# Attention then feed-forward on one core: longer score bursts, regrouped tail products, single PSUM banks and crossbar transposes

## The chip, the cores and the metric

One core of a Trainium2 chip runs one program. Times are device microseconds of an execution; most executions of a kernel agree within 0.3% to 1%. Lower is better. Every run here that is compared is of the fast state; one run of the kernel before took 1890.24 us and is left out of every comparison.

TensorE (PE) does matmuls and writes PSUM; VectorE (DVE) and ScalarE (ACT) evict PSUM; GpSimd (POOL) issues the loads, SyncE (SP) the stores and, in the changed kernel, the crossbar transposes. Each engine runs its instructions in program order (run 6 shows one holding up its queue for 4.72 us).

## The reference

```python
def _attn_ref(q, k, v):                          # (8 batches, 12 heads, 448 rows, 64)
    scores = (1 / np.sqrt(64)) * np.matmul(q, k.transpose(0, 1, 3, 2))
    attn = np.maximum(scores, 0.0) ** 2 / 448
    return np.matmul(attn, v)

def _moe_ref(x, w_gate, w_val, w_out):           # x (3584, 768), d_ff 1536
    return (np.maximum(x @ w_gate, 0.0) * (x @ w_val)) @ w_out
# reference: x is the attention result, heads side by side; output (3584, 768) float32
```

## The kernel before

Everything on TensorE is bf16. A *group* is four heads of a batch; there are 24. Per group: 28 small transposes of q and k on TensorE (T), seven score tiles S(0) to S(6), relu and square on ACT and DVE, then the products with v (PV). S(0) to S(5) use 64 rows x 128 columns of the array; S(6), the *tail* (448 = 3 x 128 + 64), uses 64x64 pieces. The main products use 128x64, their tails 64x64, feed-forward the whole 128x128. A small planner in the kernel simulates the engines and emits all instructions in the order of its planned starts. It puts *bursts* of attention between the feed-forward matmuls of the batch before.

```python
    def bank_pair(dt=FP32):          # all of PSUM: four pairs of banks, shared by every use
        return psum.tile([128, 2, 512 if dt == FP32 else 1024], dt, name="ps", tag="ps", bufs=4)
# ... cut ...
        def pv(self):                # main products, then the tail products
            for j in range(2):
                for c in range(NC):
                    for h2 in range(2):  # 12 matmuls, 128 rows x 64 columns
                        nc.tensor.matmul(x_ps[o, j, :S], ..., start=(c == 0), stop=False)
            for j, h2, half in ((0, 0, 0), (0, 1, 1), (1, 0, 1), (1, 1, 0)):
                nc.tensor.matmul(x_ps[o, j, :S], ..., start=False, stop=True)   # 64x64
# ... cut: gate and value of feed-forward share one pair, so do the two output halves ...
        nb += 1                      # nb counts bursts: four for a group
        att.append((qd.s(0), nb))
        att.append((qd.s(1), nb))
        nb += 1
        att.append((qd.s(2), nb))
        if not early: PV()           # of the group before; "early" is batch 0
        nb += 1
        att.append((qd.s(3), nb))
        if early: T(n + 1)
        att.append((qd.s(4), nb))
        if not early: T(n + 1)       # of the next group
        nb += 1
        att.append((qd.s(5), nb))
        if early: PV()
        att.append((qd.s(6), nb))
```

Of the kernel before, what the change touches and what calls it, by code (L numbers as in the profile page):

```python
# [12 lines left out]
ET = mybir.EngineType  # L13

# [17 lines left out]
class Op:  # L32
    def __init__(self, engs, emit, deps=(), alloc=(), reads=(), xfer=0.0):
        self.engs, self.emit = engs, emit
        self.deps, self.alloc, self.reads = list(deps), list(alloc), list(reads)
        self.xfer = xfer
        self.start = self.end = None


class Planner:  # L40
# [4 lines left out]
    def __init__(self):  # L45
        self.t = {}
        self.ops = []
        self.dmaq = 0.0
        self.landed = []

    def ready(self, op):
        r = 0.0
        for d in op.deps:
            if d.end is None:
                return None
            r = max(r, d.end + self.LAT)
        need = {}
        for b in op.alloc:
            need[b.res] = need.get(b.res, 0) + 1
        for res, n in need.items():  # L60
            if len(res.free) < n:
                return None
            r = max(r, sorted(res.free)[n - 1] + self.LAT)
        return r
# [12 lines left out]
    def commit(self, op, s, e):  # L77
# [4 lines left out]
        if op.xfer:  # L82
            if e == "POOL":
                self.dmaq = max(self.dmaq, op.end + 1.0) + op.xfer
                op.end = self.dmaq + 1.0
                self.landed.append(op.end)
            else:
                op.end += 2.0 + op.xfer
# [11 lines left out]
def plan(att, ffn, others, pool, nburst):  # L100
# [9 lines left out]
    while ai < len(att) or fi < len(ffn) or pend or pi < len(pool):  # L110
        cands = []
        for op in pend:
            b = P.best(op)
            if b is not None:
                cands.append((b[0], b[2], 1, b[1], op))
        if pi < len(pool):
            b = P.best(pool[pi])
            if b is not None:
# [3 lines left out]
                cands.append((s, 0.0, 0, "POOL", pool[pi]))  # L122
# [14 lines left out]
        if pick == "A":  # L137
            cands.append((A[0], A[2], 2, "PE", att[ai][0]))
        elif pick == "F":
            cands.append((F[0], F[2], 2, "PE", ffn[fi][1]))  # L140
        assert cands, "no operation can start"
        s, _, kind, e, op = min(cands, key=lambda c: c[:3])
# [23 lines left out]
def kernel(  # L166
# [36 lines left out]
    inp = ctx.enter_context(tc.tile_pool(name="inp", bufs=2))  # L203
    tpool = ctx.enter_context(tc.tile_pool(name="tpool", bufs=4))
# [8 lines left out]
    r_in, r_ps = Res(2), Res(4)  # L213
    r_t, r_r, r_at, r_x, r_h, r_g, r_o = Res(4), Res(4), Res(2), Res(2), Res(1), Res(4), Res(3)

    def bank_pair(dt=FP32):
        return psum.tile([128, 2, 512 if dt == FP32 else 1024], dt, name="ps", tag="ps", bufs=4)
# [9 lines left out]
    def dma_in(dst, src, n_desc, xfer, deps=(), alloc=()):  # L227
        op = Op({"POOL": 0.5 + 0.0004 * n_desc}, lambda: nc.gpsimd.dma_start(out=dst(), in_=src),  # L228
                deps=deps, alloc=alloc, xfer=xfer)
# [5 lines left out]
    def load_gv(c):  # L235
# [3 lines left out]
        wg_op[c] = dma_in(lambda: w_gate_sb[c], wg[:, :, cols], 768, 2.0)  # L239
        wv_op[c] = dma_in(lambda: w_val_sb[c], wv[:, :, cols], 768, 2.0)  # L240

    def load_out(c):
        wo = moe_w_out.rearrange("(kf p) m -> p kf m", p=128)
        wo_op[c] = dma_in(lambda: w_out_sb[c], wo[:, :, c * OH:(c + 1) * OH], 1536, 6.0)
# [11 lines left out]
    def load_heads(b, h0, n):  # L256
        if b not in bat:
            bat[b] = Batch()
            bat[b].buf = Buf(r_in, 1)
# [3 lines left out]
        def tiles():  # L263
            if not hasattr(st, "qk"):
                st.qk = inp.tile([128, H, NT, D], BF16, name="qk")
                st.vv = inp.tile([128, H, NC + 2, D], BF16, name="vv")
            return st
# [3 lines left out]
        al = [st.buf] if h0 == 0 else []  # L271
        k_op = dma_in(lambda: tiles().qk[64:128, hs], rows(k), 64 * n, 64 * n * 0.06 / 16, alloc=al)
        q_op = dma_in(lambda: st.qk[0:64, hs], rows(q), 64 * n, 64 * n * 0.06 / 16)
        v0 = dma_in(lambda: st.vv[0:64, hs, 1:NC + 2], rows(v)[:, :, 0:NC + 1], 64 * n, 64 * n * 0.045 / 16)
        v1 = dma_in(lambda: st.vv[64:128, hs, 0:NC + 1], rows(v)[:, :, NC:NT], 64 * n, 64 * n * 0.045 / 16)
        for h in range(h0, h0 + n):
            st.qk_op[h] = (k_op, q_op)
            st.v_op[h] = (v0, v1)
# [14 lines left out]
    def transpose_quad(b, g):  # L293

        st = bat[b]
        ps = Buf(r_ps, 2)
        box = {}

        def emit():
            t_ps = bank_pair(BF16)  # L300
            for j in range(2):
                for i, t in enumerate(slot_order(b)):
                    for h2 in range(2):
                        nc.tensor.transpose(t_ps[64 * h2:64 * h2 + 64, j, i * 128:(i + 1) * 128],  # L304
                                            st.qk[:, 4 * g + 2 * j + h2, t, :], ident)
            box["ps"] = t_ps

        def emit_copy(cp, j):
            box[j] = tpool.tile([128, 2, NT, P2], BF16, name="qk_sb")
            dst = box[j].rearrange("p a t c -> p t a c")  # L310
            src = box["ps"][:, j, :2 * S].rearrange("p (t a c) -> p t a c", t=NT, a=2)
# [6 lines left out]
        op = Op({"PE": 1.05}, emit, deps=deps, alloc=[ps])  # L318
        for j in range(2):
            sb = Buf(r_t, NC + 1)  # L320
            cp = Op({"DVE": 0.68, "ACT": 0.9}, None, deps=[op], alloc=[sb], reads=[ps])
# [11 lines left out]

    xop = {}

    class Quad:
# [6 lines left out]
        def s(self, i):  # L343
            b, g, box = self.b, self.g, self.box
            ps = Buf(r_ps, 1)
# [4 lines left out]
            def emit():  # L350
                if i == 0:
                    box["at"] = apool.tile([128, 2 * NC + 1, 2, S], BF16, name="at")
                s_ps = bank_pair()
                if i < 2 * NC:
                    _, q_of, k_of, _ = tr[0]
                    for h2 in range(2):
                        nc.tensor.matmul(s_ps[:, h2, :S], lhsT=k_of(h2, key_off(b) + (i % NC) * 128, 128),  # L357
                                         rhs=q_of(h2), start=True, stop=True)
                else:

                    for j, h2, half in ((0, 0, 0), (0, 1, 1), (1, 0, 1), (1, 1, 0)):
                        _, q_of, k_of, _ = tr[j]
                        nc.tensor.matmul(s_ps[64 * half:64 * half + 64, h2, :S],  # L363
                                         lhsT=k_of(h2, key_tail(b), P2), rhs=q_of(h2),
                                         start=True, stop=True)
                loc["s"] = s_ps

            op = Op({"PE": 0.25 if i < 2 * NC else 0.32}, emit, deps=[x[0] for x in tr],
                    alloc=[ps] + ([self.at_buf] if i == 0 else []), reads=[])
            for x in tr:  # L370
                sbuf = x[3]
                op.reads.append(sbuf)
            r = Buf(r_r, 1)

            def emit_relu(op_relu):
                loc["r"] = rpool.tile([128, 2, S], BF16, name="r_sb")
                if op_relu.eng == "ACT":
                    nc.scalar.activation(loc["r"], loc["s"][:, :, :S], AF.Relu)  # L378
                else:
                    nc.vector.tensor_scalar_max(loc["r"], loc["s"][:, :, :S], 0.0)  # L380

            relu = Op({"ACT": 0.92, "DVE": 1.12}, None, deps=[op], alloc=[r], reads=[ps])
            relu.emit = lambda: emit_relu(relu)
            sq = Op({"DVE": 0.63}, lambda: nc.vector.tensor_tensor(box["at"][:, i], loc["r"], loc["r"], ALU.mult),  # L384
                    deps=[relu], reads=[r])
            others.extend([relu, sq])
# [3 lines left out]
        def pv(self):  # L390
            b, g, box = self.b, self.g, self.box
            st = bat[b]
            ps = Buf(r_ps, 1)
            loc = {}

            def emit():
                x_ps = bank_pair()
                at = box["at"]
                for j in range(2):
                    for c in range(NC):  # L400
                        for h2 in range(2):
                            o = slice(64 * h2, 64 * h2 + 64)
                            nc.tensor.matmul(x_ps[o, j, :S], lhsT=st.vv[:, 4 * g + 2 * j + h2, 1 + c, :],  # L403
                                             rhs=at[:, NC * j + c, h2, :], start=(c == 0), stop=False)
                for j, h2, half in ((0, 0, 0), (0, 1, 1), (1, 0, 1), (1, 1, 0)):
                    p = slice(64 * half, 64 * half + 64)
                    o = slice(64 * h2, 64 * h2 + 64)
                    nc.tensor.matmul(x_ps[o, j, :S], lhsT=st.vv[p, 4 * g + 2 * j + h2, (NC + 1) * (1 - half), :],  # L408
                                     rhs=at[p, 2 * NC, h2, :], start=False, stop=True)
# [5 lines left out]
                    reads=[self.at_buf] + ([st.buf] if last else []))  # L415
# [20 lines left out]
    def ffn_ops(b):  # L436
# [8 lines left out]
        for mf in range(KF):  # L445
# [3 lines left out]
            def emit_g(loc=loc, c=c, o=o):  # L449
                loc["ps"] = bank_pair()  # L450
                loc["g"] = loc["ps"][:, 0, :S]
# [4 lines left out]
            def emit_relu(loc=loc):  # L456
                loc["gs"] = gpool.tile([128, S], BF16, name="g_sb")
                nc.scalar.activation(loc["gs"], loc["g"], AF.Relu)  # L458

            def emit_v(loc=loc, c=c, o=o):  # L460
                loc["v"] = loc["ps"][:, 1, :S]
# [4 lines left out]
            def emit_mul(loc=loc, mf=mf):  # L466
                if mf == 0 and b % 2 == 0:
                    hs["hT"] = hpool.tile([128, KF, 2 * S], BF16, name="hT")
                nc.vector.tensor_tensor(hs["hT"][:, mf, t0:t0 + S], loc["v"], loc["gs"], ALU.mult)  # L469

            ps, gs = Buf(r_ps, 2), Buf(r_g, 1)
            gop = Op({"PE": 1.15}, emit_g, deps=xop[b] + [wg_op[c]], alloc=[ps], reads=[st.x_buf])
            grel = Op({"ACT": 0.55}, emit_relu, deps=[gop], alloc=[gs], reads=[ps])
            vop = Op({"PE": 1.15}, emit_v, deps=xop[b] + [wv_op[c]], reads=[st.x_buf])
            vmul = Op({"DVE": 0.63}, emit_mul, deps=[vop, grel],
                      alloc=[hs["buf"]] if mf == 0 and b % 2 == 0 else [], reads=[ps, gs])
# [5 lines left out]
        for ti in tiles:  # L482
            obuf, ps = Buf(r_o, 1), Buf(r_ps, 2)
            cps = []
            ol = {}
            for hf in range(2):
                loc = {}

                def emit_o(ti=ti, hf=hf, loc=loc, ol=ol):
                    if hf == 0:  # L490
                        ol["ps"] = bank_pair()
                    loc["o"] = ol["ps"][:, hf, :OH]
# [4 lines left out]
                def emit_oc(cp, hf=hf, loc=loc, ol=ol):  # L497
# [5 lines left out]
                    else:  # L503
                        nc.vector.tensor_scalar_mul(dst, loc["o"], float(out_scale))

                op = Op({"PE": 1.97}, emit_o, deps=hs["mul"] + [wo_op[hf]], alloc=[ps] if hf == 0 else [],
                        reads=[hs["buf"]])
                cp = Op({"ACT": 0.5, "DVE": 0.55}, None, deps=[op] + cps, alloc=[obuf] if hf == 0 else [], reads=[ps])
# [22 lines left out]
    for g in range(NQ):  # L531
        load_heads(0, 4 * g, 4)
    id_op = Op({"POOL": 0.6}, lambda: make_identity(nc, ident))
    pool_ops.insert(2, id_op)
    for c in range(d_ff // WC):
        load_gv(c)
        if c % 2 == 0:
            load_heads(1, 2 * c, 4)
    load_out(0)
    load_out(1)  # L540
    for b in range(2, B):
        load_heads(b, 0, H)
# [6 lines left out]
    def T(n):  # L549
        if n < len(quads):  # L550
# [3 lines left out]
    for n, qd in enumerate(quads):  # L554
        prev = quads[n - 1] if n > 0 else None
        early = qd.b == 0

# [7 lines left out]
        att.append((qd.s(0), nb))  # L565
        att.append((qd.s(1), nb))
        nb += 1
        att.append((qd.s(2), nb))
        if not early:
            PV()  # L570
        nb += 1
        att.append((qd.s(3), nb))
        if early:
            T(n + 1)
        att.append((qd.s(4), nb))
        if not early:
            T(n + 1)
        nb += 1
        att.append((qd.s(5), nb))
        if early:  # L580
            PV()
        att.append((qd.s(6), nb))
# [42 lines left out]
```

## Time and profile before

| | before |
|---|---|
| time | 467.62 and 469.29 us in the two fast runs when the prediction was made (467.45 to 470.9 over all later fast runs) |
| span of the profiled run | 467.2 us |
| PE busy | 446.3 us, 96% |
| feed-forward begins | 35.98 us |
| last matmul ends | 462.1 us |

From the page of the kernel before: the busy line (us, share of the span, instructions), PE's busy tenths and granted clock in 40 slices of the span, and the chain that ended last, by engine:

```profile
PE 446.3 (96%) x3264; PEld 225.7 (48%) x3264; DVE 207.8 (44%) x323; ACT 229.8 (49%) x334; POOL 45.5 (10%) x68
...
PE   3769999999999999999999999999999999999995
...
PEclk9899999999999999999999999999999999999999
...
PE 90%; DMA 6%; issue 1%; ACT 1%; POOL 1%; ACTq 0%; POOLq 0%
```

PE is the bottleneck, and at a full clock (9 is 90% or more) after the beginning. Where it is *not* full is seen in the windows view. Columns: window, its length, then busy us and instruction count of each engine, granted PE clock, DMA share, GB/s:

```profile
0.00:36.00 36.00, 21.08 (x247) 11.82 (x248) 21.51 (x34) 23.80 (x28) 23.38 (x40) 0.92 1.25 175
36.00:462.00 426.00, 425.08 (x3020) 213.88 (x3018) 186.33 (x289) 205.17 (x304) 22.07 (x29) 1.00 0.39 69
```

From 36 to 462 us PE lacks 0.9 us. So there are three parts: a beginning of 36 us in which PE works 21 us, a middle of 426 us in which only less PE work helps, and an end of 5 us with the last eviction and store.

The timeline of PE, one burst of the kernel before (start us, duration us, engine, line, operation, operands, rows*columns of the array, shapes, count). Durations contain the pipeline's latency; the cost of a piece is the distance from its start to the next start:

```profile
103.93 0.36 PE L357 MATMUL ps<-qk_sb 64*128 64x448 bf16 x2
104.22 1.33 PE L403 MATMUL ps<-at,vv 128*64 128x448 bf16 x12
105.47 0.38 PE L408 MATMUL ps<-at,vv 64*64 64x448 bf16 x4
105.79 1.31 PE L463 MATMUL ps<-xT,wv_99 128*128 128x448 bf16 x6
```

The two score matmuls here cost 104.22 - 103.93 = 0.29 us, where such a pair costs 0.19 us when the shape does not change after it. Each change of shape costs about 0.1 us in this way.

The transposes, from the table of groups of the kernel before (line, engine, operation, operands, shapes, count | busy us, mean ns of one | idle before and what ended it):

```profile
L304 PE MATMUL ps<-ident,qk 128*64 128x128 bf16 x672 | 26.3, 236 | 11.1 <-DMA qk<-in_q_dram 10.1 <-ACT r_sb L378 1.0
```

They are busy for 26.3 us; in the timeline the 28 of a group take 0.91 us from start to start. The last is the end of the beginning, in PE's timeline of the kernel before:

```profile
30.69 0.55 PE L357 MATMUL ps<-qk_sb 64*128 64x448 bf16 x4
34.35 1.71 PE L304 MATMUL ps<-ident,qk 128*64 128x128 bf16 x28 [3.10 <-DMA qk<-in_q_dram]
35.98 1.30 PE L453 MATMUL ps<-xT,wg_91 128*128 128x448 bf16 x3
```

PE waits 3.10 us for q of batch 1, because the transposes of a later group stand before the feed-forward in its program.

### The profile page before, as it was taken

Reading aid. Unit: us, or ns where it says so; the run is one execution under the profiler, and the core shown is the slowest. Engines: PE = TensorE matmul, PEld = TensorE weight load, DVE = VectorE, ACT = ScalarE, POOL = GpSimd, SP = SyncE. Lnnn points to the kernel's source line nnn. Section 1 sums busy time; section 2 is a strip of 40 time slices with the busy share of each in tenths; the row PEclk is TensorE's granted clock in tenths of the full one; section 3 lists DMA queues with packets and bytes.
Section 4 is the critical chain, followed back from the end, with each engine's and each line's share of the span. In section 5 each row is a group of like instructions: output and inputs, shape, how many; then the busy total and the mean of one; then the engine's idle time right before and its main releaser. Section 6 shows DMA issues by size and latency. Waiting matters only on the chain.

```text
span 467.2 us, 7638 instructions
## 1 busy us (share of the span) xinstructions
PE 446.3 (96%) x3264; PEld 225.7 (48%) x3264; DVE 207.8 (44%) x323; ACT 229.8 (49%) x334; POOL 45.5 (10%) x68
## 2 busy tenths in 40 slices
PE   3769999999999999999999999999999999999995
PEld 2334445544455445554455444554445544455553
DVE  1975454545533554454642645454553345502210
ACT  3984554555635455445553555455563464632221
POOL 8645200101001010000101010010000000000000
PEclk9899999999999999999999999999999999999999
DMA  9999999614327070260714416160002200021013
GB/s 128 197 198 198 203 204 194 100 37 60 59 69 135 2 111 8 69 102 0 120 34 93 78 20 99 35 106 30 1 1 67 69 2 0 1 69 34 1 34 102
DMA packets 42371, 35.88 MB, mean 77 GB/s; under 512 B 1889, under 2 KB 38753, under 8 KB 42337
## 3 DMA queue, kind: packets, MB, share of 16 engines
q0 software_dynamic: 37856, 24.38, 36.7%
q1 hardware_dynamic: 4480, 11.01, 8.8%
q8 instruction: 25, 0.41, 0.4%
q14 instruction: 10, 0.07, 0.0%
HBM read 48.76 MB, written 11.01 MB: 128 GB/s over the span
## 4 chain that ended last, share of the span: by engine, by line
PE 90%; DMA 6%; issue 1%; ACT 1%; POOL 1%; ACTq 0%; POOLq 0%
PE ps L453 24%; PE ps L463 24%; PE ps L494 23%; PE ps L357 6%; DMA qk<-in_q_dram 6%; PE ps L403 6%; PE ps L304 4%; PE ps L408 1%; PE ps L363 1%; ACT g_sb L458 1%; POOL qk L228 0%; POOL vv L228 0%; ACT r_sb L378 0%; POOL wv_97 L228 0%; ACT o_sb L502 0%
## 5 line engine op out<-in xcount | busy, mean ns | idle before, releaser
L384 DVE TENSOR_TENSOR at<-r_sb 128x896 bf16<-128x896 bf16 x168 | 101.2, 621 | 42.7 <-ACT r_sb L378 41.8
L378 ACT ACTIVATE r_sb<-ps 128x896 bf16<-128x896 f32 x134 | 118.1, 925 | 3.8 <-PE ps L357 3.8
L458 ACT ACTIVATE g_sb<-ps 128x448 bf16<-128x448 f32 x96 | 52.3, 545 | 127.7 <-PE ps L463 113.1
L469 DVE TENSOR_TENSOR hT<-ps,g_sb 128x448 bf16<-128x448 f32 x96 | 59.9, 624 | 121.2 <-ACT g_sb L458 105.5
L494 PEld LDWEIGHTS <-hT 128*128 128x128 bf16 x672 | 63.7, 98 | 45.9 <-issue 5.2
L380 DVE TENSOR_SCALAR r_sb<-ps 128x896 bf16<-128x896 f32 x34 | 37.1, 1091 | 56.8 <-PE ps L357 33.1
L502 ACT ACTIVATE o_sb<-ps 128x384 f32<-128x384 f32 x56 | 24.9, 490 | 73.7 <-PE ps L494 70.6
L494 PE MATMUL ps<-wo_103,hT 128*128 128x384 bf16 x336 | 59.4, 327 | 0.2 <-ACT r_sb L378 0.2
L494 PE MATMUL ps<-wo_104,hT 128*128 128x384 bf16 x336 | 59.2, 326 | 0.0
L357 PE MATMUL ps<-qk_sb 64*128 64x448 bf16 x288 | 44.8, 366 | 3.4 <-ACT r_sb L378 1.2
L304 PE MATMUL ps<-ident,qk 128*64 128x128 bf16 x672 | 26.3, 236 | 11.1 <-DMA qk<-in_q_dram 10.1
L403 PE MATMUL ps<-at,vv 128*64 128x448 bf16 x288 | 32.0, 358 | 0.4 <-ACT r_sb L378 0.4
L304 PEld LDWEIGHTS <-qk 128*64 128x64 bf16 x672 | 22.3, 120 | 19.8 <-issue 19.8
L228 POOL DMA_DIRECT2D vv<-in_v_dram x24 | 16.4, 692 | 151.7 <-PE ps L408 149.3
L313 ACT COPY qk_sb<-ps 128x896 bf16<-128x896 bf16 x24 | 21.9, 912 | 16.3 <-DVE qk_sb L315 9.1
L357 PEld LDWEIGHTS <-qk_sb 64*128 64x128 bf16 x288 | 10.6, 95 | 35.6 <-issue 33.5
L422 ACT CAST xT<-ps 128x896 bf16<-128x896 f32 x23 | 21.0, 913 | 11.0 <-PE ps L408 11.0
L315 DVE COPY qk_sb<-ps 128x896 bf16<-128x896 bf16 x24 | 14.9, 621 | 19.2 <-ACT qk_sb L313 16.0
L453 PE MATMUL ps<-xT,wg_91 128*128 128x448 bf16 x96 | 21.4, 361 | 0.0
L463 PE MATMUL ps<-xT,wv_101 128*128 128x448 bf16 x96 | 20.8, 352 | 0.3
L463 PE MATMUL ps<-xT,wv_100 128*128 128x448 bf16 x96 | 20.8, 352 | 0.3
L403 PEld LDWEIGHTS <-vv 128*64 128x64 bf16 x288 | 14.5, 110 | 13.2 <-issue 6.0
(49 smaller groups left out, 352.4 us busy)
## 6 DMA issues: line engine op xcount, KB each, us to landing
out_dram<-o_sb SPq DMA_DIRECT2D x56, 192.0 KB, 2.7
vv<-in_v_dram POOLq DMA_DIRECT2D x12, 384.0 KB, 6.6
qk<-in_k_dram POOLq DMA_DIRECT2D x6, 672.0 KB, 7.4
qk<-in_q_dram POOLq DMA_DIRECT2D x6, 672.0 KB, 10.3
vv<-in_v_dram POOLq DMA_DIRECT2D x12, 128.0 KB, 8.5
qk<-in_k_dram POOLq DMA_DIRECT2D x6, 224.0 KB, 8.0
qk<-in_q_dram POOLq DMA_DIRECT2D x6, 224.0 KB, 8.6
wo_103<-in_moe_w_out_dram POOLq DMA_DIRECT2D x1, 1152.0 KB, 14.3
```

The source lines that it names most:

```text
L304: nc.tensor.transpose(t_ps[64 * h2:64 * h2 + 64, j, i * 128:(i + 1) * 128], st.qk[:, 4 * g + 2 * j + h2, t, :], ident)
L357: nc.tensor.matmul(s_ps[:, h2, :S], lhsT=k_of(h2, key_off(b) + (i % NC) * 128, 128), rhs=q_of(h2), start=True, stop=True)
L378: nc.scalar.activation(loc["r"], loc["s"][:, :, :S], AF.Relu)
L380: nc.vector.tensor_scalar_max(loc["r"], loc["s"][:, :, :S], 0.0)
L384: sq = Op({"DVE": 0.63}, lambda: nc.vector.tensor_tensor(box["at"][:, i], loc["r"], loc["r"], ALU.mult), deps=[relu], reads=[r])
L403: nc.tensor.matmul(x_ps[o, j, :S], lhsT=st.vv[:, 4 * g + 2 * j + h2, 1 + c, :], rhs=at[:, NC * j + c, h2, :], start=(c == 0), stop=False)
L453: nc.tensor.matmul(loc["g"], lhsT=w_gate_sb[c][:, kd, o:o + 128], rhs=st.xT[:, kd, :], start=(kd == 0), stop=(kd == KD - 1))
L458: nc.scalar.activation(loc["gs"], loc["g"], AF.Relu)
L463: nc.tensor.matmul(loc["v"], lhsT=w_val_sb[c][:, kd, o:o + 128], rhs=st.xT[:, kd, :], start=(kd == 0), stop=(kd == KD - 1))
L469: nc.vector.tensor_tensor(hs["hT"][:, mf, t0:t0 + S], loc["v"], loc["gs"], ALU.mult)
L494: nc.tensor.matmul(loc["o"], lhsT=hs["hT"][:, kf, ti * 128:(ti + 1) * 128], rhs=w_out_sb[hf][:, kf, :], start=(kf == 0), stop=(kf == KF - 1))
L502: nc.scalar.activation(out=dst, in_=loc["o"], func=AF.Copy, scale=float(out_scale))
```

## The change

The intent: give PE less to do, and fewer changes of shape.

- Three bursts for a group: S(0,1,2), S(3,4,5), and S(6) with the products of the group before; the tail products come first in them, next to S(6), as both are 64x64.
- PSUM is split: two pairs of banks for scores and products, four single banks for feed-forward, transposes, and the first tile of each long burst, whose relu becomes two halves.
- q and k of batches 3 to 7 are transposed by the DMA crossbar: seven DVE copies put head pairs side by side, then two DMA transposes from SBUF to SBUF.
- Loads come in smaller pieces and another order, v apart from q and k; in batch 0 the order of the attention pieces changes too.

```diff
+XBAR_FROM = 3
@@ planner: priorities, a delay after loads, other transfer times (cut)
-    def bank_pair(dt=FP32):
-        return psum.tile([128, 2, 512 if dt == FP32 else 1024], dt, name="ps", tag="ps", bufs=4)
+    def bank_pair():
+        return psum.tile([128, 2, 512], FP32, name="s_ps", tag="s", bufs=2)
+
+    def bank(name, dt=FP32):
+        return psum.tile([128, 512 if dt == FP32 else 1024], dt, name=name, tag="f", bufs=4)
@@ new: crossbar transposes of one batch (shortened)
+    def transpose_batch(b):
+        def emit_pair(s, t):                      # seven of these, on DVE
+            if s == 0:
+                box["p"] = pairs.tile([128, HP, NT, 2, D], BF16, name="pair")
+            nc.vector.tensor_copy(box["p"][:, :, s], st.qk[:, :, t, :].rearrange("p (a c) d -> p a c d", c=2))
+            op = Op({"DVE": 0.28}, lambda s=s, t=t: emit_pair(s, t), deps=deps + perm[:1], delay=6.0,
+                    alloc=[pair] if s == 0 else [], reads=[st.buf])
+        def emit_x(i):                            # two of these, for q and for k
+            nc.sync.dma_start_transpose(
+                out=box["x"][i].rearrange("p a (t c) -> p (a t) c", c=P2),
+                in_=box["p"][64 * i:64 * i + 64].rearrange("p a t c d -> p (a t c d)"))
+            op = Op({"SP": 0.3}, lambda i=i: emit_x(i), deps=perm + xo[:1], alloc=[xb] if i == 0 else [],
+                    reads=[pair], xfer=10.0)
@@ class Quad
-        def s(self, i):
+        def s(self, i, split=False):
-            ps = Buf(r_ps, 1)
+            single = split and i < 2 * NC
+            ps = [Buf(r_f, 1), Buf(r_f, 1)] if single else [Buf(r_s, 1)]
@@ pv: the four tail products move before the twelve main ones (start=True), cut
@@ feed-forward: gate, value and each output half get a single bank, cut
@@ load order (cut), then the sequence
         nb += 1
-        att.append((qd.s(0), nb))
-        att.append((qd.s(1), nb))
+        S_(0, 1, 2)                               # the first of three tiles is split
         nb += 1
-        (S(2), PV, S(3), T, S(4), S(5), S(6) in three more bursts)
+        if early and not last_early:
+            T(n + 1)
+        S_(3, 4, 5)
+        nb += 1
+        S_(6)
+        if early:
+            PV()
+        if last_early:                            # last group of batch 0
+            nb += 1
+            att.append((qd.pv(), nb))
+            xburst[0] = nb
+            T(n + 1)
+        elif not early:
+            if n != NQ:
+                PV()
+            T(n + 1)                              # nothing for batches 3 to 7
```

## The prediction

> **What bounds it now.** TensorE. The page gives PE 96% of a 467.2 us span; the chain of waits is 90% PE, 6% the loads of q. By the windows view PE is over 99.7% busy at full clock from 36 to 462 us; before 36 us it is busy for 21 us, at clock 0.92; after 462 us come only the last eviction and store (5 us). DVE (44%) and ACT (49%) have room. The middle gets shorter only if PE gets less to do or pays less between pieces.
>
> **What PE pays.** In the timeline, start to start, feed-forward matmuls of 448 columns come every 189 ns, pairs of score matmuls every 187 ns. Each change of array shape costs about 0.1 us more: feed-forward to 64-row scores 96 ns, scores to products 103 ns, tail to feed-forward 125 ns, out of the transposes 158 ns. The Trainium skill, "TensorEngine Tiling (Array Packing)", Key Properties, says that changing the mode drains TensorE; the trace agrees, with these numbers. A group of four heads has four bursts and 12 such changes; after 45 us they sum to about 31 us, 1.5 us a group.
>
> **What the change removes.**
> 1. Bursts: three-tile bursts, tail scores and tail products in one mode, then products and any transposes in one mode: 3 bursts, 7 changes. Costed as above 0.8 us a group, so 0.7 us x 21 groups = about 15 us, all critical.
> 2. Transposes of batches 3 to 7: 15 of 24 groups. Each takes 0.91 us start to start, about 0.78 without the shape change already counted: about 12 us, all critical. Their 30 evictions (0.62 us DVE, 0.91 ACT) hide behind PE.
> 3. Start: PE waits 3.1 us at 31-34 us for q of batch 1, then transposes; feed-forward starts at 36 us. The new load order and later transpose let it start near 32.5 us; two score tiles and a transpose move into the middle: net 2 us. The phase before stays bound by ACT and DVE.
>
> **What it adds.** 35 DVE pair copies, estimated 0.3-0.6 us each from the 0.62 us copy: hidden. Ten crossbar transposes of 0.69 MB: the Trainium skill, "DMA: Bandwidth & Descriptors", Latency and other measured facts, gives 261 GB/s, so an estimate of 2.6 us each; nothing in this trace shows one, and I allow 10 us. They are due a batch later (50 us): hidden, unless they hold up the stores on their queue; three output buffers, refilled every 3.9 us, give some 8 us of slack. Splitting a burst's first tile adds 0.2 us of eviction 48 times, off the path. Single banks: no credit, as PE isn't waiting for banks.
>
> **Sum.** 467.2 - 15 - 12 - 2 = 438 us of span, about 440 as timed. I add 4 us for new waits: a burst needs three tiles' banks at once. Prediction 444 us, range 436 to 456; faster by over 2%: 0.90, within 2%: 0.07, slower: 0.03.
>
> **What would show it.** PE busy down to about 420 us, no PE idle over 1 us after 36 us; 252 transposes instead of 672; about 7 shape changes a group, each still near 0.1 us; feed-forward from 31-34 us; the same 5 us tail.
>
> **What would prove it wrong.** PE idle before score bursts, ended by ACT or DVE: two bank pairs and four singles are too few. PE waiting for transposed q or k, or for output evictions behind a store: the crossbar is much slower than allowed. Feed-forward later than 36 us: loads bound the beginning. Shape changes dearer in the new orders would eat step 1.

## The result

| | before | changed |
|---|---|---|
| median time of the fast runs, us | 469.29 (467.62 to 469.8) | 448.75 (445.38 to 449.94) |
| ratio | | 0.9559, 95% interval 0.9483 to 0.9634 |
| span of the profile, us | 467.2 | 447.8 |
| feed-forward begins | 35.98 | 35.60 |
| middle: from there to the end of the last matmul | 426.1 | 407.2 |
| end, after the last matmul | 5.1 | 5.0 |

A ratio is the mean time of one kernel's fast runs over that of the other's fast runs of the same rounds, so it is not quite the ratio of the medians quoted. The same lines of the page of the changed kernel:

```profile
PE 425.3 (95%) x2844; PEld 212.8 (48%) x2844; DVE 224.4 (50%) x376; ACT 205.9 (46%) x334; POOL 45.5 (10%) x68
...
PE   2679999999989998999999999999999999999995
...
PEclk9979999999999999999999999999999999999999
```

And its windows, cut at its own last matmul:

```profile
0.00:36.00 36.00, 21.87 (x211) 10.92 (x212) 18.43 (x31) 20.98 (x29) 21.42 (x36) 0.91 1.22 166
36.00:442.00 406.00, 402.69 (x2632) 201.57 (x2631) 205.99 (x346) 184.44 (x305) 24.08 (x32) 1.00 0.55 90
```

All of the gain is in the middle, and there PE now lacks 3.3 us of 406. One third burst of a group, in PE's timeline of the changed kernel:

```profile
140.46 0.38 PE L422 MATMUL s_ps<-qT,kT 64*64 64x448 bf16 x4
140.67 0.36 PE L468 MATMUL s_ps<-at,vv 64*64 64x448 bf16 x4
140.96 1.33 PE L474 MATMUL s_ps<-at,vv 128*64 128x448 bf16 x12
142.22 2.12 PE L561 MATMUL o_ps<-wo_109,hT 128*128 128x384 bf16 x12
```

And the transposes that are left on PE, from its table of groups:

```profile
L314 PE MATMUL t_ps<-ident,qk 128*64 128x128 bf16 x252 | 11.0, 251 | 8.8 <-DMA qk<-in_q_dram 8.8
```

S(6) and the tail products follow each other with almost no extra cost (140.46 to 140.67 is 0.21 us; a pair of score matmuls of the same 448 columns takes 0.19). TensorE does 252 transposes instead of 672. But the beginning did not get shorter, although PE's wait for q of batch 1 has gone. PE's timeline of the changed kernel at the end of the beginning:

```profile
29.72 2.45 PE L474 MATMUL s_ps<-at,vv 128*64 128x448 bf16 x12
...
32.62 2.26 PE L474 MATMUL s_ps<-at,vv 128*64 128x448 bf16 x12
...
35.60 1.31 PE L518 MATMUL g_ps<-xT,wg_97 128*128 128x448 bf16 x6
```

The two product groups take 2.45 and 2.26 us here, and 1.33 us for the same 12 matmuls elsewhere (the fence above). And there are two new waits. One is for the transposed k of batch 3. In the changed kernel's timeline, the first and last of the six loads on POOL (the four between are cut), the issue of the transpose of k on SP, and PE's scores that wait for it:

```profile
104.41 0.74 POOL L235 DMA_DIRECT2D qk<-in_k_dram  x1 [39.44 <-DVE pair L355]
...
108.08 0.80 POOL L235 DMA_DIRECT2D qk<-in_q_dram  x1
...
108.35 11.22 SPq L367 DMA_TRANSPOSE kT<-pair  x1
...
131.10 0.74 PE L416 MATMUL s_ps<-qT,kT 64*128 64x448 bf16 x6 [2.12 <-DMA kT<-pair]
```

The table of DMA issues in that window has the time from issue to landing in its last column:

```profile
qT<-pair SPq DMA_TRANSPOSE x1, 11.9
kT<-pair SPq DMA_TRANSPOSE x1, 22.7
```

The other wait, 1.2 us at 170 us, is for a DVE multiplication that stood behind a late pair copy on DVE.

So after the first comparison the theory was: fewer shape changes and fewer transposes shorten the middle as forecast; the 2.1 us wait comes from the crossbar meeting the six loads (issues at 104.4 to 108.9 us); the beginning loses its gain to a half clock. The rivals: the gain comes chiefly from one part; single banks do nothing, as forecast, or are what makes the bursts possible; the slow beginning is a matter of loads and evictions.

### The profile page after: what moved, and what is told of

Same layout as the page of the kernel before. It is cut to its first block, busy times and chain, and to the rows that moved or that the text cites. A ratio compares the mean times of both kernels' runs of the same rounds, so it can differ in the third digit from the quotient of the medians.

```text
span 447.8 us, 7021 instructions
## 1 busy us (share of the span) xinstructions
PE 425.3 (95%) x2844; PEld 212.8 (48%) x2844; DVE 224.4 (50%) x376; ACT 205.9 (46%) x334; POOL 45.5 (10%) x68
## 4 chain that ended last, share of the span: by engine, by line
PE 88%; DMA 7%; ACT 2%; issue 1%; DVE 1%; POOL 1%; SPq 0%; ACTq 0%; DVEq 0%; POOLq 0%
PE o_ps L561 24%; PE g_ps L518 23%; PE v_ps L531 23%; PE s_ps L474 7%; PE s_ps L416 6%; DMA kT<-pair 5%; PE s_ps L422 2%; DMA qk<-in_q_dram 2%; ACT r_sb L432 1%; PE t_ps L314 1%; PE s_ps L468 1%; POOL qk L235 1%; DVE at L450 0%; SPq L367 0%; DVE qk_sb L325 0%
## 5 line engine op out<-in xcount | busy, mean ns | idle before, releaser
L432 ACT ACTIVATE r_sb<-s_ps 128x448 bf16<-128x448 f32 (+1 forms) x148 | 100.3, 737 | 34.6 <-PE s_ps L416 22.5
L537 DVE TENSOR_TENSOR hT<-v_ps,g_sb 128x448 bf16<-128x448 f32 x96 | 59.9, 624 | 106.7 <-PE v_ps L531 105.6
L524 ACT ACTIVATE g_sb<-g_ps 128x448 bf16<-128x448 f32 x96 | 52.4, 546 | 107.0 <-PE g_ps L518 107.0
L434 DVE TENSOR_SCALAR r_sb<-s_ps 128x896 bf16<-128x896 f32 (+1 forms) x68 | 60.9, 921 | 43.2 <-PE s_ps L416 43.0
L569 ACT ACTIVATE o_sb<-o_ps 128x384 f32<-128x384 f32 x56 | 27.5, 491 | 72.1 <-PE o_ps L561 72.1
L561 PE MATMUL o_ps<-wo_109,hT 128*128 128x384 bf16 x336 | 59.3, 327 | 0.0
L561 PE MATMUL o_ps<-wo_110,hT 128*128 128x384 bf16 x336 | 59.2, 326 | 0.0
L474 PE MATMUL s_ps<-at,vv 128*64 128x448 bf16 x288 | 33.9, 374 | 0.0
L416 PE MATMUL s_ps<-qT,kT 64*128 64x448 bf16 x180 | 22.6, 352 | 3.3 <-DMA kT<-pair 2.1
L518 PE MATMUL g_ps<-xT,wg_97 128*128 128x448 bf16 x96 | 20.8, 353 | 0.0
L518 PE MATMUL g_ps<-xT,wg_101 128*128 128x448 bf16 x96 | 20.8, 353 | 0.0
L518 PE MATMUL g_ps<-xT,wg_99 128*128 128x448 bf16 x96 | 20.8, 353 | 0.0
L518 PE MATMUL g_ps<-xT,wg_102 128*128 128x448 bf16 x96 | 20.8, 353 | 0.0
L518 PE MATMUL g_ps<-xT,wg_100 128*128 128x448 bf16 x96 | 20.8, 353 | 0.0
L531 PE MATMUL v_ps<-xT,wv_104 128*128 128x448 bf16 x96 | 20.8, 353 | 0.0
L518 PE MATMUL g_ps<-xT,wg_98 128*128 128x448 bf16 x96 | 20.8, 353 | 0.0
L531 PE MATMUL v_ps<-xT,wv_106 128*128 128x448 bf16 x96 | 20.8, 353 | 0.0
```

The costliest lines, as they stand in the source:

```text
L416: nc.tensor.matmul(half_of(h2), lhsT=k_of(h2, key_off(b) + (i % NC) * 128, 128), rhs=q_of(h2), start=True, stop=True)
L432: nc.scalar.activation(dst, src, AF.Relu)
L434: nc.vector.tensor_scalar_max(dst, src, 0.0)
L474: nc.tensor.matmul(x_ps[o, j, :S], lhsT=st.vv[:, 4 * g + 2 * j + h2, 1 + c, :], rhs=at[:, NC * j + c, h2, :], start=False, stop=(c == NC - 1))
L518: nc.tensor.matmul(loc["g"], lhsT=w_gate_sb[c][:, kd, o:o + 128], rhs=st.xT[:, kd, :], start=(kd == 0), stop=(kd == KD - 1))
L524: nc.scalar.activation(loc["gs"], loc["g"], AF.Relu)
```

## The experiments

Twelve runs. "Middle" is from the first feed-forward matmul to the end of the last matmul of the profile; it keeps the beginning's chances out of the comparison. The last column lists waits of PE over 1 us after 36 us.

| run | median us (range) | ratio to before | feed-forward begins | middle us | waits |
|---|---|---|---|---|---|
| changed, first | 448.75 (445.38 to 449.94) | 0.9559 | 35.60 | 407.2 | 2.1 k, 1.2 DVE |
| 1 no crossbar | 456.63 (453.77 to 457.66) | 0.9715 | 34.84 | 415.2 | none |
| 2 four bursts | 453.83 (453.22 to 455.72) | 0.9672 | 33.22 | 413.6 | none |
| 3 bank pairs | 460.53 (459.86 to 462.21) | 0.9813 | 32.31 | 420.5 | many of 0.3 to 0.7 |
| 4 crossbar only | 459.09 (457.62 to 460.56) | 0.9787 | 31.17 | 419.2 | 2.2 k |
| 5 changed again | 450.67 (449.7 to 451.14) | 0.9610 | 35.31 | 408.2 | 2.4 k |
| 6 pairs early | 447.93 (445.05 to 448.21) | 0.9543 | 32.35 | 405.9 | 2.3 DVE |
| 7 warm | 450.23 (449.25 to 452.93) | 0.9609 | 36.33 | 406.5 | 2.2 k |
| 8 warm and early | 450.01 (449.44 to 451.5) | 0.9602 | 34.98 | 407.7 | 2.5 DVE |
| 9 early, longer plan | 444.88 (443.06 to 447.3) | 0.9481 | 34.03 | 403.7 | none |
| 10 light warm | 448.56 (446.11 to 452.08) | 0.9557 | 33.22 | 405.9 | 1.9 k |
| 11 early, light warm | 442.81 (442.5 to 443.04) | 0.9434 | 32.49 | 403.7 | none |
| 12 tails last | 452.99 (450.98 to 455.96) | 0.9655 | 35.04 | 409.2 | 1.9 k |

Runs 1 to 4, 5 to 8 and 9 to 12 each shared a chip and its runs of the kernel before (medians 469.1, 469.16 and 469.55 us), so that ratios are comparable. All runs gave the right result. The edits below are against the changed kernel.

### Which part gives what

**Run 1, no crossbar.**

```diff
-XBAR_FROM = 3
+XBAR_FROM = 8
```

> The changed kernel, but every batch is transposed on TensorE (672 transposes again, no crossbar). Theory: the 15 transposes of groups cost 0.75 to 0.80 us each on TensorE, 11 to 12 us, and the 2.1 us wait for the transposed k of batch 3 goes away, so about +9.5 us over the changed kernel: 456 to 460 us. Rival: the crossbar gives most of its gain back by crowding the loads; then this run is within 4 us of the changed kernel (under 453 us).

456.63 us. The middle is 11.5 us longer than in run 9, which has everything and no wait (415.2 against 403.7); two transposes start every 56 ns in the trace, so the 28 of a group take 0.78 us and 15 groups 11.7 us. Against the changed kernel itself, 8.0 us in the middle, because that one pays for its waits. So the theory holds, and the crossbar as built gave back 3.5 us of it in waits.

**Run 2, four bursts.** The old four bursts from batch 1 on, and the old product order in all batches, batch 0 too; banks, crossbar and the rest of batch 0 as changed. In the five groups that still have transposes they stand between S(3) and S(4), and not after S(4) as in the kernel before: one more change of shape in each.

```diff
@@ sequence of a group from batch 1 on; each nb += 1 begins a burst
-            nb += 1; S_(0, 1, 2)
-            nb += 1; S_(3, 4, 5)
-            nb += 1; S_(6); PV(); T(n + 1)
+            nb += 1; S_(0, 1)
+            nb += 1; S_(2); PV()
+            nb += 1; S_(3); T(n + 1); S_(4)
+            nb += 1; S_(5); S_(6)
@@ pv: the twelve main products first, the four tails last
```

> The changed kernel with the old four bursts of a group and the tail products last again, from batch 1 on; crossbar, single banks and batch 0 as changed. Theory: 11 shape changes a group instead of 7 (batches with crossbar transposes), each 0.10 to 0.11 us, over 21 groups: about +9 us, 455 to 460 us, TensorE never idle for longer than in the changed kernel. Rival: the changes of shape are hidden or the long bursts themselves cost waits; then it is within 3 us of the changed kernel.

453.83 us, just under the range, and 5.1 us over the changed kernel instead of 9; but its profile has a beginning at full clock and none of the changed kernel's waits. In the middle it is 9.9 us longer than run 9, which has no waits either, for a forecast of 9. The starts in PE's timeline show where. Take the time from the start of each piece to the start of the next, less what its matmuls need when they follow each other (189 ns for a feed-forward matmul of 448 columns, a pair of scores or products or four tail matmuls, 162.5 ns for a feed-forward matmul of 384 columns, 56 ns for two transposes: the usual distances in these traces, for the tails an assumption). Over the whole middle these joints (all but feed-forward to feed-forward) cost 28.0 us before, 26.0 us here and 16.3 us in run 9. The theory holds. By the same count the "about 31 us" of the prediction was somewhat high.

**Run 3, bank pairs.** Three-tile bursts and crossbar on the old PSUM layout: four shared pairs, no split tile, gate and value in one pair.

```diff
-        return psum.tile([128, 2, 512], FP32, name="s_ps", tag="s", bufs=2)
+        return psum.tile([128, 2, 512 if dt == FP32 else 1024], dt, name="s_ps", tag="s", bufs=4)
@@ bank() and r_f are gone; every use takes a pair from r_s = Res(4)
```

> The changed kernel with the PSUM layout of before: four shared pairs of banks for everything, feed-forward gate and value in one pair, no split tile. Theory (as predicted: TensorE was not waiting for banks): within 3 us of the changed kernel, 445 to 452 us. Rival: single banks are what makes three-tile bursts possible; a burst takes three of four pairs, so feed-forward waits for an eviction after each of about 42 such bursts, 0.3 to 0.6 us each: +12 to +25 us, 460 to 474 us, with TensorE idle ended by ACT or DVE.

460.53 us: the rival is right. PE's busy time is that of the changed kernel (423.4 and 425.3 us); the rest is idle time after the bursts. One of them in the timeline of this run, with the relu of the gate, the multiplication and the feed-forward matmuls that wait:

```profile
109.07 0.74 PE L410 MATMUL s_ps<-qk_sb 64*128 64x448 bf16 x6
109.23 0.54 ACT L519 ACTIVATE g_sb<-s_ps 128x448 bf16<-128x448 f32 x1 [1.77 <-PE s_ps L526]
...
109.80 0.62 DVE L532 TENSOR_TENSOR hT<-s_ps,g_sb 128x448 bf16<-128x448 f32 x1 [1.70 <-ACT g_sb L519]
...
110.48 1.29 PE L513 MATMUL s_ps<-xT,wg 128*128 128x448 bf16 x6 [0.67 <-DVE hT L532]
```

The burst takes three of four pairs, and the fourth still holds the value tile, which waits for relu and multiplication. Over the 40 long bursts after 45 us the way from scores back to feed-forward costs 20.7 us over streaming, against 4.4 us in the changed kernel (one wait inside a burst left out).

The number of tiles is not all that this run undoes. When gate and value share a pair, the relu of the gate begins only after the matmuls of the value, 1.17 us (median) after the gate is ready; with single banks it begins 0.04 us after the gate. The tables of groups show it in what ended ACT's idle time before the relu, here (L526 is the value) and in the changed kernel (L518 is the gate):

```profile
L519 ACT ACTIVATE g_sb<-s_ps 128x448 bf16<-128x448 f32 x96 | 52.2, 544 | 147.7 <-PE s_ps L526 142.6 <-PE s_ps L513 5.1
...
L524 ACT ACTIVATE g_sb<-g_ps 128x448 bf16<-128x448 f32 x96 | 52.4, 546 | 107.0 <-PE g_ps L518 107.0
```

No run separates the two, so what is shown is that the whole bank layout matters, not the count of tiles alone.

**Run 4, crossbar only.** Runs 2 and 3 combined: old bursts, old products, old banks; only crossbar, loads and batch 0 are new.

> The kernel before plus only the crossbar for batches 3 to 7 and the new load order and batch 0 order (old four bursts, old product order, old shared bank pairs). Theory: about 11 us under the kernel before, less a wait or two for the crossbar: 457 to 461 us, and the same as the four-burst run with single banks within 3 us. Rival: the parts do not add up and this alone gives nearly all of the gain (under 452 us) or nearly none (over 466 us).

459.09 us, as expected of the time. It is not within 3 us of run 2 (5.3 us above): 2.2 us of that is the wait for k, which this order has and that of run 2 has not, and the rest small waits for banks that run 2 does not have. Together the four runs show how the parts combine: on shared pairs, long bursts are worth nothing (runs 3 and 4: 460.5 and 459.1, although run 4 has 2.2 us of waiting for k in it); on single banks they are worth 10 us of the middle (run 2 against run 9).

**Run 12, tails last.** Only the order inside the products undone.

> The changed kernel with the tail products after the others, as in the kernel before: one more change of array shape in each group (7 become 8), 0.10 to 0.13 us each, over 21 groups. Theory: 2 to 3 us over the unaltered kernel's 450.7 us: 452.5 to 454 us. Rival: the order of the tail is worth nothing: within 1 us of 450.7 us.

452.99 us, 2.3 us over run 5, and by the ratios 0.0045 x 469 = 2.1 us. The size fits, but the intervals touch (0.9586 to 0.9634 for run 5, 0.9621 to 0.9689 here), and the chips differ; so the times are agreement, not proof. The starts in the two profiles show the cost itself: from the tail scores through the products to feed-forward, the joints of a group cost 0.12 us more here (0.39 against 0.27 us), 2.5 us over 20 groups.

### The wait for the transposed k

**Run 5, the changed kernel again**, as the reference.

> The changed kernel once more, unaltered, as the reference of this chip and to see its own spread: 445 to 450 us. Theory: the spread comes from the granted clock around 27 to 36 us, which is half in some runs (the first profile: products of 12 matmuls took 2.45 us, feed-forward from 35.6 us) and full in others (then 1.33 us, feed-forward from about 33.3 us). Rival: the spread lies elsewhere, and feed-forward starts at the same time in every profile.

450.67 us, just above the range; half clock again at the beginning of its profile (the lines stand under run 11), and feed-forward at 35.31 us. Its clock (third from the end) fell once more, right after the 2.4 us wait for k at 131 us:

```profile
132.00:135.40 3.40, 3.40 (x13) 1.54 (x12) 2.75 (x5) 0.84 (x2) 0.00 (x0) 0.50 1.10 241
```

The feed-forward matmuls after it took 1.7 us longer than in the first profile for this, so here a wait cost nearly twice its own length. Run 8 has the same after its wait of 2.45 us; the six other profiles with waits of 1.9 to 2.3 us have not.

**Run 6, pairs early.** The pair copies come first on DVE as soon as the data has landed.

```diff
-            op = Op({"DVE": 0.28}, ..., deps=deps + perm[:1], delay=6.0,
-                    alloc=[pair] if s == 0 else [], reads=[st.buf])
+            op = Op({"DVE": 0.28}, ..., deps=deps + perm[:1], delay=1.0,
+                    alloc=[pair] if s == 0 else [], reads=[st.buf], prio=0)
```

> The changed kernel with the pair copies on VectorE issued as soon as q and k have landed, ahead of other work, so that the crossbar transposes of batch 3 are issued near 90 us and not at 104 and 108 us. Theory: the 2.1 us wait of TensorE at 129 us for the transposed k goes away and perhaps the 1.2 us one at 169 us: 2 to 3 us under the unaltered run beside it. Rival: the transposes are slow by themselves or meet the same loads, and a wait of 1 us or more for the transposed k stays.

447.93 us. The wait for k is gone, with the transpose of k issued at 93.6 us. But another wait came in, which neither theory had. The timeline of this run, DVE and PE:

```profile
115.65 0.36 DVE L356 COPY pair<-qk 128x768 bf16<-128x768 bf16 x1 [4.72 <-DMA kT<-pair]
115.92 0.62 DVE L538 TENSOR_TENSOR hT<-v_ps,g_sb 128x448 bf16<-128x448 f32 x1
...
116.59 1.29 PE L532 MATMUL v_ps<-xT,wv 128*128 128x448 bf16 x6 [2.30 <-DVE hT L538]
```

A pair copy of batch 4 sat 4.72 us at the head of DVE's queue until the transpose of batch 3 had read the buffer; the multiplication of feed-forward stood behind it, and PE behind that. The transpose still takes about 22 us; only its place has moved. The loads have moved with it: the first of them waits for the buffer that the pair copies of batch 3 set free, as its releaser shows, here on POOL in run 6 and at 104.41 us in the changed kernel:

```profile
87.47 0.74 POOL L236 DMA_DIRECT2D qk<-in_k_dram  x1 [25.75 <-DVE pair L356]
```

So the same copies start the transposes and the loads that meet them.

**Run 9, early and a longer plan.** As run 6, and the planner is told 14 us for a transpose.

```diff
-                    reads=[pair], xfer=10.0)
+                    reads=[pair], xfer=14.0)
```

> The run with early pair copies, and the plan told that a crossbar transpose takes 14 us and not 10, so that the pair copies of batch 4 come later in VectorE's program. In the run with early copies alone, one of them sat 4.7 us at the head of VectorE's queue, waiting for the transpose of batch 3, and TensorE lost 2.3 us at 114 us behind it. Theory: that wait goes, about 2 us under the run with early copies alone: 445 to 447 us, and TensorE has no wait over 1 us after 36 us. Rival: the wait moves once more to another place and the time stays at 448 us.

444.88 us, a little better than expected. The crossbar is no faster; the planner only no longer puts work behind it that others need. From the view of the tile of head pairs in this run (duration ns of the issue, minimum, median and maximum, first and last start; then the time to landing):

```profile
L368 SPq DMA_TRANSPOSE kT<-pair x5: 4354/5296/11272, 95.7 to 285.6; - x5
...
DMA to landing us min/median/max: 6.5/7.0/21.6
```

And the windows view of this run from 36 us to its last matmul:

```profile
36.00:438.00 402.00, 401.76 (x2627) 200.92 (x2625) 204.95 (x344) 183.58 (x305) 23.85 (x32) 1.00 0.54 90
```

PE lacks 0.2 us of 402.

The wait was thus a matter of order, not of bandwidth alone. That the 22 us come from the loads in flight, and not from the first transpose being slow as such, can be read from the transpose of k of batch 4. In the changed kernel it was issued at 148.01 us with four loads in flight for 18.2 us of its time; in run 6 it was issued at 130.68 us and had landed before the next load was issued at 139.62 us. Issue to landing, in the table of DMA issues of the changed kernel from 147 to 167.5 us and of run 6 from 130 to 138.5 us:

```profile
kT<-pair SPq DMA_TRANSPOSE x1, 18.9
...
kT<-pair SPq DMA_TRANSPOSE x1, 7.3
```

In the changed kernel, the other transposes of batches 4 to 7 had loads beside them for 3.2 us at most and landed in 6.4 to 8.8 us. The Trainium skill says why it can be ("DMA: Bandwidth & Descriptors", Issuing engines are not separate DMA queues: DMAs of all issuers run on the same 16 engines and interleave). No run moved only the loads away, and none did so for batch 3; that loads in flight make a transpose slow is shown by batch 4, how they share the engines is not.

### The beginning

The Trainium skill, "TensorE: Matmul & The Clock Gate", Part 1, The HAM clock gate, says that half clock is the array's default, that a busy window of about 3.4 us releases it and an idle one brings it back. It says too that these windows run free of the program's start. The traces agree in the length: in their records of the clock every fall before the end lasts 3.41 or 6.83 us. In the changed kernel's batch 0 PE is busy little more than half of the time between 21 and 30 us. In runs with the very same order of batch 0 on PE, ACT and DVE the clock fell after 21 us (profiles of the first run and of runs 1, 5 and 9) or did not (run 6), and feed-forward began at 34.0 to 35.6 us or at 32.35 us. With the tail products last in batch 0 it fell in run 12 (35.04 us) and not in run 2 (33.22 us). The kernel before is not free of it: its clock was 0.63 from 33 to 36 us. In run 6 the one execution with mean clock 0.999 took 445.05 us, the five with 0.992 to 0.995 took 447.3 to 448.21 us; where in those five it fell is not on record.

**Run 7, warm.** Four matmuls of no use before each of the seven score tiles of group 2 of batch 0, into a bank that is never read.

```diff
+            warm = b == 0 and g == 2
+                if warm:
+                    w_ps = bank("w_ps")
+                    _, q_of, k_of, _ = tr[0]
+                    for _ in range(4):
+                        nc.tensor.matmul(w_ps[:, :S], lhsT=k_of(0, 0, 128), rhs=q_of(0), start=True, stop=True)
```

> The changed kernel with four more matmuls of no use (into a spare bank, never read) before each of the seven score tiles of group 2 of batch 0, about 0.75 us each, where TensorE was half idle. Theory: granted clock stays at 1.0 from 24 to 36 us in every profile, the two product groups take 1.33 us each, feed-forward starts at 33 to 34 us; the median 0.5 to 2 us under the unaltered run, and its spread narrower. Rival: the beginning is bound by the evictions on ACT and DVE and by the loads; then the extra matmuls only delay it, and the median is the same or up to 3 us higher.

450.23 us: no gain. Both sides were half right. The products took 1.33 us and the clock was 1.00 from 27 us on; but 28 matmuls at about 0.19 us are 5.3 us, more than the idle time there was, and feed-forward began at 36.33 us.

**Run 8, both.** Runs 6 and 7 together.

> Both edits of this call together. If both theories hold, they add: 3 to 5 us under the unaltered run, 443 to 445 us, with no idle of TensorE over 1 us after 36 us. If one of them fails, as that one alone.

450.01 us: they did not add up. The clock stayed at 1.00 throughout 15 to 36 us, but feed-forward began at 34.98 us, and the new wait behind the pair copy (2.5 us) was there as in run 6. After this wait the clock fell to 0.50 from 119.3 to 122.7 us, which it did not in run 6; that is most of the 1.8 us by which the middle is longer than in run 6.

**Run 10, light warm.** Only where PE waits anyway: 16 matmuls.

```diff
-            warm = b == 0 and g == 2
+            warm = {(0, 1, 6): 6, (0, 2, 2): 2, (0, 2, 4): 3, (0, 2, 6): 5}.get((b, g, i), 0)
```

> The changed kernel with extra matmuls only where TensorE waits anyway in batch 0: 6 before the last tile of group 1; 2, 3 and 5 before the third, fifth and last tile of group 2 (16 of 187 ns, 3 us in all, instead of 28). Theory: as these fill idle time, feed-forward is not delayed and the granted clock stays at 1.0 to 36 us: feed-forward from 32.3 to 33.7 us, 1 to 2.5 us under the unaltered kernel's 450.7 us: 448 to 450 us. Rival: the clock falls all the same, or the extra work delays the start, and the time is 450 us or more.

448.56 us, from 446.11 to 452.08. In the profile the clock is 1.00 from 15 to 36 us and feed-forward begins at 33.22 us; but two of the six runs have a mean clock of 0.987, so in these it fell, here or, as in runs 5 and 8, after the wait for k, which is still 1.9 us. By itself this run is inconclusive: its interval (0.9521 to 0.9594) overlaps that of run 5.

**Run 11, early copies, longer plan and light warm.**

> The edits of the two runs before this one, together. If both hold: 443 to 445.5 us. If only the first: as the first.

442.81 us, just under the range, four runs within 0.6 us, ratio 0.9434 (0.9410 to 0.9458), the fastest here; run 9 on the same chip has 0.9481 (0.9449 to 0.9512). PE's busy time (third column) and the granted clock (third from the end) in 3 us windows, first of run 5, the changed kernel again:

```profile
24.00:27.00 3.00, 2.54 (x14) 0.69 (x11) 1.29 (x3) 1.89 (x3) 2.42 (x4) 0.63 1.45 196
27.00:30.00 3.00, 1.09 (x8) 0.41 (x8) 3.00 (x6) 2.91 (x6) 0.80 (x2) 0.94 1.45 197
30.00:33.00 3.00, 2.98 (x20) 1.13 (x19) 1.43 (x3) 0.77 (x1) 1.26 (x2) 0.50 1.45 197
```

Then of this run, and from 36 us to its last matmul:

```profile
24.00:27.00 3.00, 2.71 (x19) 1.16 (x17) 2.54 (x4) 2.96 (x6) 2.06 (x3) 1.00 1.45 197
27.00:30.00 3.00, 2.33 (x23) 0.99 (x21) 2.99 (x6) 2.33 (x3) 0.96 (x2) 1.00 1.45 197
30.00:33.00 3.00, 3.00 (x51) 1.91 (x48) 0.40 (x1) 2.08 (x3) 1.10 (x2) 1.00 1.45 197
```

```profile
36.00:436.00 400.00, 400.00 (x2619) 200.28 (x2618) 204.32 (x343) 183.37 (x304) 23.75 (x32) 1.00 0.54 91
```

The extra matmuls raise PE's busy time to 2.3 us and more of each 3 us, the clock stays at 1.00 through these windows, and from 36 us to the last matmul PE is never idle. Even here the clock fell once, to 0.50 between 18 and 21 us of the same profile, where it did no visible harm. So that the half clock costs some 2 us is shown by the runs with one order; that filling the idle time cures it is supported by runs 9 and 11 (the slowest of run 11 is just below the fastest of run 9, though the intervals of their ratios touch) and not by run 10 alone.

## Why the prediction was right

The time was 448.75 us, inside 436 to 456 and 4.75 us above the 444 forecast. The main mechanism, less work and fewer shape changes in a middle in which PE is busy throughout, was right. The errors of the steps did not cancel: about 3.3 us each from steps 1 and 3, and the range was wide enough for them. By steps, as the prediction numbered them:

1. *Bursts, about 15 us.* The joints between pieces fell from 28.0 to 16.3 us (run 9), by 11.7 us: right, somewhat over-sized. There are 146 changes after 45 us, 7 a group, as said.
2. *Transposes, about 12 us.* 11.5 us by run 1 against run 9, 11.7 us by the starts: right.
3. *Start, 2 us.* This step failed in the first profile. The order of loads did take PE's wait for q away, but the forecast took "the phase before stays bound by ACT and DVE" for the whole story. As PE is half idle in it, its clock can fall, and the two product groups at the end, which *are* on the critical path, then took 2.45 and 2.26 us for 1.33. Feed-forward began at 35.6 and not 32.5 us. In runs with a full clock it did begin at 32.4 to 33.2 us (runs 6, 2 and 10). What moved into the middle was also more than said: five score tiles and a group's transposes, 1.7 us, and not two tiles.
4. *New waits, 4 us.* The profile has two over 1 us, 2.1 and 1.2 us. The size was right by luck, as the cause was not the one named: not banks, but the crossbar's landing and a DVE queue held up by it. The transposes were allowed 10 us and did land in 6.4 us at best, but in 22.7 us when six loads were in flight.
5. *Single banks: no credit.* Nearly true of the kernel before (PE lacks 0.9 us of its middle), but wrong for the new order: without them the long bursts are worth nothing (run 3 is 10 to 12 us slower). A resource that nothing waits for in the old order can be what the new order needs.

The sum closes. In the middle, 426.1 us less 11.7 (joints) less 11.7 (transposes) less 0.6 (small waits between feed-forward matmuls) plus 1.7 (a group's transposes, 0.8, and five score tiles, 0.9, moved from the beginning into it) is 403.8 us; run 9 measured 403.7, and the changed kernel 407.2 with its 3.3 us of waits.

The signs named beforehand: transposes 252, shape changes 7, end 5 us came true; PE busy is 425.3 us for "about 420"; "no idle over 1 us after 36 us" and "feed-forward from 31 to 34 us" did not hold, and both name what was then found.

## What to carry to other kernels

When PE is the bottleneck at full clock, count its changes of array shape and price them from the distance between starts in the timeline; regrouping them is worth real time, but only with PSUM banks enough that the longer burst does not wait for evictions. When a transfer is moved off PE, look at what stands *behind* its consumers in each in-order queue, and plan with its landing time beside other transfers, not its best one; ask also which transfers the same instructions set free. A wait can cost more than its length, when PE's clock falls after it. And if a phase is bound by another engine, check PE's granted clock there before taking its later work at full speed.

## What the Trainium skill lacked or had wrong

- "DMA: Bandwidth & Descriptors", Latency and other measured facts: 261 GB/s for a DMA transpose with a non-contiguous middle dimension. In the changed kernel an SBUF-to-SBUF transpose of 64 x 5376 bf16 (0.69 MB) landed 6.4 us after its issue began at best, which is 108 GB/s (3.9 us of it are the issue on SP's queue, so the two are not the same measure), and in 22.7 us beside six loads. As an estimate of the time to landing the figure was too fast here by more than two; the measurement decides.
- "TensorEngine Tiling (Array Packing)", Key Properties: a change of mode drains TensorE, without a number. Here 94 to 159 ns over streaming, with 448-column matmuls and 128-column transposes.
- "TensorE: Matmul & The Clock Gate", Why this matters for your kernels: no idle gaps over about 3 us between bursts. That is not enough here: in run 5 no idle of PE from 15 to 33 us was longer than 2.02 us, and the clock still fell to 0.50 in 30 to 33 us; and it fell after single waits of 2.40 and 2.45 us in runs 5 and 8, but not after 2.30 us in run 6. Another section of the page, A second HAM failure mode, does say that frequent short idling makes the clock oscillate. Neither says what share of busy time holds the clock: in 24 to 27 us, 1.2 us busy of 3 us held it in run 6, and 1.8 us did not in the first profile, where it was 0.62 in the next 3 us.
